# Batch 0's first two token chunks by seven half products, and block-by-block waits for the sums of w_out

## The chip, the core and the metric

The kernel runs on one core of one Trainium2 chip. The metric is the device time of one execution in microseconds (us). The core has five engines that matter here, each with its own in-order queue of instructions: PE (TensorE: matmuls, with the weight loads, PEld, beside them), DVE (VectorE), ACT (ScalarE), POOL (GpSimd) and SP (SyncE, which only issues transfers). An instruction waits at the head of its queue until the semaphores that it names have been raised by others; nothing behind it on that engine starts before it.

## The reference

```python
scores = (1 / sqrt(64)) * q @ k.transpose      # 8 batches, 12 heads, 448 tokens, head size 64
attn   = relu(scores) ** 2 / 448
x      = (attn @ v), heads side by side        # 3584 tokens x 768
h      = x @ w_in                              # w_in 768 x 2048
g      = relu(h) ** 2
out    = g @ w_out                             # w_out 2048 x 768, out 3584 x 768 in float32
```

The inputs come in float32; the kernel casts them to float16 and accumulates in float32.

## The kernel before, in words

**Tiles and stages.** A batch has 448 tokens and 3 units of 4 heads (24 units in all). For each unit, q and k are loaded, cast and turned (`turn_pe` on PE for units 0 to 5, `turn_dma` L476 as a transposing transfer on SP from unit 6 on). A round is one seventh of a unit's keys: `scores` (L522, eight small matmuls of 64x64 tiles for two rounds), then `squared`: the relu out of PSUM into a buffer `rel` (L538 on DVE or L541 on ACT), and its square into `at` (L545 on ACT or L548 on POOL). After seven rounds `av` (L588, 28 small matmuls) gives x, which L608 or L610 writes as `xt`. Then the dense part: `h_group` (L650, six matmuls of 128x128 over 448 columns for each of 16 blocks of w_in; `h_first` at L699 and `h_part` for batch 0), evacuated by ACT (L639, square) and DVE (L634, mask) into `g`.

**The output products.** A token chunk is 128 tokens of `g`, 16 blocks deep. w_out lies in four blocks `w2[hf][i]`: columns `hf` (LO or HI 384), rows `i` (the first or the second 1024). In the names of the code b11 = `w2[0][0]`, b21 = `w2[0][1]`, b12 = `w2[1][0]`, b22 = `w2[1][1]`. One chunk done plainly (`plain_groups`, L799) is two groups of 16 matmuls of 384 columns, one for each half of the columns. Two chunks together can be done by `o_groups` with seven half products (L864), m1 to m7, of 8 such matmuls each, in place of eight: a Strassen-Winograd scheme. It needs four sums of `g` (`combine`, L843, on DVE: s1 to s4) and four sums of w_out (`combine_w2`: t1 = b12-b11, t2 = b22-t1, t4 = t2-b21, and t3 = b22-b12, which is written over b12), each sum of w_out in two halves, on DVE (L828) or POOL (L825). The products' results are put together by ACT copies (L783; L785 is its form on DVE) and DVE additions (`close`, L876), and stored by SP (L745). In the kernel before, 13 of the pairs are done so, and only the first two chunks of batch 0 are plain (`PLAIN0 = True`); since t3 overwrites b12, it waits there for the plain products.

**What sets the order.** The order of each queue is not written by hand. `Plan` records every operation with costs, dependencies, buffers and a due time, then simulates the engines (`simulate`, `pick`: of the operations that are ready, the one with the earliest due time) under 16 pairs of settings (`PATIENCE`, how long PE may idle before a filler matmul, L1009, is put in, and `LEAD`), keeps the best and emits it. `push_dense` queues the dense work of a batch: its 16 h groups mixed with `QUOTA[b]` products that are left over or new; `run_some` spreads that queue between the score rounds. So a small edit can move instructions everywhere. The waits in the emitted program follow from the data that an instruction really touches; the dependencies given to `Plan` only say when the plan takes an operation to be ready.

**Loads.** w_in comes in four transfers on POOL's queue (L496), w_out in four (`load_w2`, L501), in the order of the string `ORDER`, in which w0 to w3 are `w2[0][0]`, `w2[0][1]`, `w2[1][0]`, `w2[1][1]`. On the same queue lie v (L489) and the early q and k (L406). From unit 6 on, q and k are loaded by SP (L389) into four `raw` buffers and cast by POOL (L440) into three `blk` buffers. Where a DVE sum (L828, L843) holds the port that DVE shares with POOL, the next POOL operation of the plan is made to wait for it (`behind`).

Of the kernel before, what the change touches and what calls it, by code (L numbers as in the profile page):

```python
# [297 lines left out]
def kernel(  # L298
# [35 lines left out]
    def fixed(pool, name, n, shape, dt):  # L334
        return [pool.tile(shape, dt, name=f"{name}{i}", tag=f"{name}{i}") for i in range(n)]

    w1 = fixed(sb, "w1_", 4, [P, NM, 512], FP16)
    w2 = [fixed(sb, f"w2_{hf}", 2, [P, NH, HALF], FP16) for hf in range(2)]
    t1, t2, t4 = fixed(sb, "wt", 3, [P, NH, HALF], FP16)
# [160 lines left out]
    def load_w2(hf, i, after, due=None):  # L500
        return plan.add([("POOL", 0.85, 0.85, lambda: nc.gpsimd.dma_start(  # L501
            out=w2[hf][i], in_=moe_w_out[1024 * i:1024 * (i + 1),
                                         hf * HALF:(hf + 1) * HALF].rearrange(
                "(f p) d -> p f d", p=P)), WQ)], after=after, due=due)
# [273 lines left out]
    def copied(op, bank, part):  # L778
        def emit(kind):
            def run():  # L780
                dst, src = part.tile, bank.tile[:, 0:HALF]
                if kind == "ACT":
                    nc.scalar.activation(out=dst, in_=src, func=AF.Copy, scale=CO)  # L783
                else:
                    nc.vector.tensor_scalar_mul(dst, src, CO)  # L785
            return run
        return plan.add([act(HALF, emit("ACT")), dve(HALF, emit("DVE"))], [op], [bank, part],
                        due=plan.now + 0.3)
# [25 lines left out]

    def combine_w2():
        (b11, b21), (b12, b22) = w2
        steps = [("t1", lambda r: (t1[:, r], b12[:, r], b11[:, r]), []),
                 ("t2", lambda r: (t2[:, r], b22[:, r], t1[:, r]), ["t1"]),
                 ("t4", lambda r: (t4[:, r], t2[:, r], b21[:, r]), ["t2"]),
                 ("t3", lambda r: (b12[:, r], b22[:, r], b12[:, r]), ["t1"])]  # L820
        for name, args, before in steps:
            t_ops[name] = [
                plan.add([("POOL", 3.06, 3.1,
                           lambda r=slice(4 * z, 4 * z + 4), args=args:
                           nc.gpsimd.tensor_sub(*args(r))),  # L825
                          ("DVE", 0.9, 0.98,
                           lambda r=slice(4 * z, 4 * z + 4), args=args:
                           nc.vector.tensor_sub(*args(r)), 0, True)],  # L828
                         [w for hf in range(2) for w in w2_ops[hf]]
                         + [t_ops[x][z] for x in before]  # L830
                         + (plain_ops if name == "t3" else []))
                for z in range(2)]

    def o_groups(one, two):
        (ready1, buf1, view1, at1), (ready2, buf2, view2, at2) = one, two
        lo, hi = slice(0, NH), slice(NH, NF)
        st: dict = {}

        def combine(name, fn, deps, srcs, x, y):
            buf = Buf("comb")  # L840

            def emit():
                return fn(buf.tile, x(), y())  # L843
            st[name] = plan.add([("DVE", 0.6, 0.68, emit, 0, True)], deps, [buf] + srcs), buf

        def sums():
            vec = nc.vector
            combine("s1", vec.tensor_add, ready2(), [buf2()],
                    lambda: view2()[:, lo], lambda: view2()[:, hi])
            combine("s2", vec.tensor_sub, ready1() + [st["s1"][0]], [buf1(), st["s1"][1]],  # L850
                    lambda: st["s1"][1].tile, lambda: view1()[:, lo])
            combine("s3", vec.tensor_sub, ready1() + ready2(), [buf1(), buf2()],
                    lambda: view1()[:, lo], lambda: view2()[:, lo])
            combine("s4", vec.tensor_sub, ready1() + [st["s2"][0]], [buf1(), st["s2"][1]],
                    lambda: view1()[:, hi], lambda: st["s2"][1].tile)

        def product(bank, lhs, deps, srcs, w, first, last=True):
            if first:
                st[bank] = Buf("mm")
            buf = st[bank]  # L860

            def emit():
                for j in range(NH):
                    nc.tensor.matmul(  # L864
                        buf.tile[:, 0:HALF], lhsT=lhs()[:, j, :], rhs=w[:, j, :],
                        start=(first and j == 0), stop=(j == NH - 1), skip_group_check=True)
            return plan.pe(0.1625 * NH, emit, deps, [buf] + srcs)

        def part(name, bank, op):
            st[name] = Buf("part")  # L870
            st[name, "op"] = copied(op, st[bank], st[name])
            return st[name, "op"]

        def close(at, cols, bank, op, name, sign=1.0):
            osb, src, r = Buf("part"), st[bank], st[name]
            done = plan.add([dve(HALF, lambda: nc.vector.scalar_tensor_tensor(  # L876
                out=osb.tile, in0=src.tile[:, 0:HALF], scalar=sign * CO, in1=r.tile,
                op0=ALU.mult, op1=ALU.add))], [op, st[name, "op"]], [src, r, osb],
                due=plan.now + 0.3)
            store(done, at, cols, osb)  # L880
            return done

        def summed(name):
            op, buf = st[name]
            return lambda: buf.tile, [op], [buf]

        def m1():
            sums()
            op = product("x", lambda: view1()[:, lo], ready1() + w2_ops[0], [buf1()],
                         w2[0][0], True)  # L890
            part("r1", "x", op)

        def m2():
            op = product("y", lambda: view1()[:, hi], ready1() + w2_ops[0], [buf1()],
                         w2[0][1], True)
            close(at1, LO, "y", op, "r1")

        def m6():
            lhs, deps, srcs = summed("s2")
            op = product("x", lhs, deps + t_ops["t2"] + [st["r1", "op"]], srcs, t2, False)  # L900
            part("r2", "x", op)

        def m5():
            lhs, deps, srcs = summed("s1")
            op = product("z", lhs, deps + t_ops["t1"], srcs, t1, True)
            part("r5", "z", op)

        def m7():
            lhs, deps, srcs = summed("s3")
            op = product("x", lhs, deps + t_ops["t3"] + [st["r2", "op"]], srcs, w2[1][0], False)  # L910
            part("r3", "x", op)
            close(at2, HI, "x", op, "r5")

        def m3():
            lhs, deps, srcs = summed("s4")
            op = product("z", lhs, deps + w2_ops[1] + [st["r5", "op"]], srcs, w2[1][1], False)
            close(at1, HI, "z", op, "r2")

        def m4():
            op = product("w", lambda: view2()[:, hi], ready2() + t_ops["t4"], [buf2()], t4, True)  # L920
            close(at2, LO, "w", op, "r3", -1.0)

        return [(0.1625 * NH, fn) for fn in (m1, m2, m6, m5, m7, m3, m4)]
# [17 lines left out]
            queued -= c  # L941
            credit -= c

    QUOTA = (4, 12, 9, 12, 12, 13, 12, 99)
    backlog: list = []

    def push_dense(b):
# [4 lines left out]
        if b == 0:  # L952
            if PLAIN0:
                both = [plain_groups(chunk(b, c)) for c in range(2)]
# [6 lines left out]
        else:  # L961
# [4 lines left out]
            new += o_groups(chunk(b, 1), chunk(b, 2))  # L966
        old = backlog[:QUOTA[b]]
        beside = max(0, len(old) - 2)
# [11 lines left out]
        backlog[:] = backlog[len(old):] + new  # L980
        now = QUOTA[b] - len(old)
        push(backlog[:now])
        del backlog[:now]
        if b == 0 and PLAIN0:
            push([(0.0, combine_w2)])

    ORDER = "u3 v3 u4 v4 u5 v5 w0 w1 w2 w3"
    EARLY = 6
    PLAIN0 = True
    NPE = 6  # L990
    MERGE = True
    ROUNDS = NUN * TJ
# [77 lines left out]
    tile(1, rounds[0:1])  # L1070
    put(0, quads[-1])
    tile(1, rounds[1:2])
    w2_ops = [[], []]
    for z, one in enumerate(ORDER.split()):
        at, n = 15.0 + 0.01 * z, int(one[1])
        if one[0] == "u":
            for w_ in "kq":
                casts[n, w_] = load_early(n, w_, 15.0, at)
        elif one[0] == "v":
            load_v(n, 15.0, at)  # L1080
        else:
            w2_ops[n // 2].append(load_w2(n // 2, n % 2, 15.0, at))
    for i in range(2, STREAM):
        tile(1, rounds[i:i + 1])
        if i % 4 == 3:
# [1 line left out]
        if i % TJ == 2 and i > TJ:  # L1087
            n = i // TJ - 1
# [12 lines left out]
    for i in range(STREAM // 2, NB):  # L1101
# [19 lines left out]
        for n, t in rs:  # L1121
            sp = [Buf("mm"), Buf("mm")]
            op = scores([(n, t)], sp, WHOLE, False)
# [4 lines left out]
        for op, sp, n, t in todo:  # L1128
            second, at = square(op, sp, S)
# [50 lines left out]
```

## Time and profile before

| what | value |
|---|---|
| six runs | 381.95 to 384.76 us, median 382.55 us |
| the profiled execution | 381.95 us |
| its span, first to last instruction | 380.2 us |
| outside the span | 1.75 us |
| granted TensorE clock, mean | 0.996 |
| fillers L1009 on PE | 20 |
| products L799 / L864 on PE | 64 / 832 matmuls |

The span is what the views show; times in the views count from its start. In the table of groups a matmul's mean is its whole passage; as matmuls are pipelined, the next one starts earlier, and what a matmul costs in a stream is the length of a run of them over their number, which the chain and the timeline give. "idle before" is the time that an engine stood still before an instruction, and the name behind the arrow is what ended it.

### The profile page before, as it was taken

What the parts mean: (1) busy time and instruction counts of PE and PEld (TensorE: products, weight loads), DVE (VectorE), ACT (ScalarE), POOL (GpSimd) and SP (SyncE); (2) the same over time, 40 slices, a digit from 0 to 9 for tenths busy, and PEclk for the clock granted to TensorE, in tenths of its full rate; (3) what the DMA queues carried; (4) which work ended last, traced back from release to release, by engine and by line L of the source; (5) the groups of instructions that cost most, each with busy time, mean ns of one, the idle gap of its engine ahead of it and who ended that gap; (6) DMA issues with size and microseconds to landing.
All of it is one profiled execution on the core that took longest, in us unless ns stands there. A gap on an engine that the chain in (4) does not pass through costs nothing.

```text
span 380.2 us, 8809 instructions
## 1 busy us (share of the span) xinstructions
PE 371.0 (98%) x3295; PEld 198.2 (52%) x3295; DVE 266.3 (70%) x468; ACT 269.8 (71%) x584; POOL 221.5 (58%) x270
## 2 busy tenths in 40 slices
PE   8889999999999999999999999999999999999995
PEld 4546555444555445544554555545555545555663
DVE  2985888786985678677986576685885668256731
ACT  5998999897767787688777686696795785244221
POOL 8999894896756668775475674974752443000100
PEclk9899999999999999999999999999999999999999
DMA  8999998996398954859368764774553002200243
GB/s 183 195 206 203 203 236 214 239 186 153 72 203 192 184 153 80 161 127 242 54 121 219 170 154 83 184 170 103 128 99 84 2 1 60 68 21 0 63 105 85
DMA packets 70219, 51.37 MB, mean 135 GB/s; under 512 B 36896, under 2 KB 70176, under 8 KB 70176
## 3 DMA queue, kind: packets, MB, share of 16 engines
q1 hardware_dynamic: 52384, 35.86, 38.1%
q0 software_dynamic: 16928, 14.09, 25.3%
q10 hardware_dynamic: 864, 0.85, 0.7%
q8 instruction: 26, 0.43, 0.5%
q14 instruction: 17, 0.14, 0.1%
HBM read 45.61 MB, written 11.01 MB: 149 GB/s over the span
## 4 chain that ended last, share of the span: by engine, by line
PE 91%; ACT 3%; POOL 2%; DMA 2%; DVE 1%; issue 0%; POOLq 0%; DVEq 0%; ACTq 0%
PE mm L650 38%; PE mm L864 32%; PE mm L522 9%; PE mm L588 8%; PE mm L799 3%; DMA g<-in_k_dram 2%; POOL at L548 1%; ACT at L545 1%; PE mm L460 1%; ACT rel L541 1%; DVE rel L538 0%; POOL g L406 0%; PE mm L699 0%; PE mm L1009 0%; ACT comb L545 0%
## 5 line engine op out<-in xcount | busy, mean ns | idle before, releaser
L548 POOL TENSOR_TENSOR at<-rel 128x448 f16<-128x448 f32 (+1 forms) x144 | 130.1, 924 | 69.3 <-DVE rel L538 52.3
L650 PE MATMUL mm<-xt,w 128*128 128x448 f16 (+1 forms) x768 | 148.7, 346 | 0.0
L634 DVE SCALAR_TENSOR_TENSOR g<-mm,g 128x448 f16<-128x448 f32 (+1 forms) x128 | 77.2, 605 | 49.9 <-ACT g L639 49.6
L650 PEld LDWEIGHTS <-w 128*128 128x128 f16 x768 | 72.5, 98 | 70.2 <-issue 11.2
L538 DVE TENSOR_SCALAR rel<-mm 128x448 f32<-128x448 f32 (+3 forms) x176 | 97.5, 596 | 13.5 <-PE mm L522 12.6
L639 ACT ACTIVATE g<-mm 128x448 f16<-128x448 f32 (+1 forms) x128 | 68.9, 539 | 46.8 <-PE mm L650 45.5
L545 ACT ACTIVATE at<-rel 128x448 f16<-128x448 f32 (+1 forms) x192 | 101.6, 590 | 0.5 <-PE mm L588 0.5
L541 ACT ACTIVATE rel<-mm 128x448 f32<-128x448 f32 (+2 forms) x172 | 83.1, 548 | 5.3 <-PE mm L522 5.1
L864 PEld LDWEIGHTS <-comb 128*128 128x128 f16 x416 | 39.6, 98 | 30.2 <-issue 4.1
L522 PE MATMUL mm<-qkt,qkt 64*64 64x448 f16 (+2 forms) x756 | 51.6, 341 | 1.1 <-DVE rel L538 0.7
L783 ACT ACTIVATE part<-mm 128x384 f32<-128x384 f32 x42 | 20.9, 498 | 43.9 <-PE mm L864 43.0
L876 DVE SCALAR_TENSOR_TENSOR part<-mm,part 128x384 f32<-128x384 f32 x52 | 28.4, 555 | 24.8 <-ACT part L783 15.0
L440 POOL CAST blk<-raw 128x896 f16<-128x896 f32 x36 | 33.5, 945 | 20.6 <-DMA raw<-in_k_dram 5.4
L864 PE MATMUL mm<-w,comb 128*128 128x384 f16 x208 | 36.7, 326 | 0.0
L864 PE MATMUL mm<-wt,comb 128*128 128x384 f16 x208 | 36.5, 326 | 0.0
L588 PE MATMUL mm<-at,vs 64*64 64x448 f16 (+1 forms) x672 | 35.8, 343 | 0.2
L864 PEld LDWEIGHTS <-g 128*128 128x128 f16 x264 | 25.4, 98 | 18.5 <-issue 1.8
L522 PEld LDWEIGHTS <-qkt 64*64 64x64 f16 x756 | 18.5, 107 | 25.1 <-issue 21.2
L489 POOL DMA_DIRECT2D vs<-in_v_dram x48 | 30.1, 633 | 1.4 <-DMA g<-in_k_dram 1.1
L765 POOL COPY rest<-g 128x1024 f16<-128x1024 f16 x8 | 8.3, 1034 | 38.7 <-DVE comb L843 35.5
L864 PE MATMUL mm<-w,g 128*128 128x384 f16 x176 | 30.8, 326 | 0.0
L588 PEld LDWEIGHTS <-vs 64*64 64x64 f16 x756 | 22.5, 110 | 14.6 <-issue 3.8
(61 smaller groups left out, 211.6 us busy)
## 6 DMA issues: line engine op xcount, KB each, us to landing
out_dram<-part SPq DMA_DIRECT2D x108, 96.0 KB, 2.2
raw<-in_k_dram SPq DMA_DIRECT2D x18, 448.0 KB, 4.1
raw<-in_q_dram SPq DMA_DIRECT2D x18, 448.0 KB, 5.0
vs<-in_v_dram POOLq DMA_DIRECT2D x48, 112.0 KB, 4.4
w<-in_moe_w_in_dram POOLq DMA_DIRECT2D x4, 768.0 KB, 12.5
w<-in_moe_w_out_dram POOLq DMA_DIRECT2D x4, 768.0 KB, 13.6
g<-in_k_dram POOLq DMA_DIRECT2D x4, 224.0 KB, 10.9
g<-in_q_dram POOLq DMA_DIRECT2D x4, 224.0 KB, 10.0
```

The costliest lines, as they stand in the source:

```text
L440: return lambda: fn(blk.tile.rearrange("p t (f d) -> p f t d", f=2), tile_of().rearrange("p f (t d) -> p f t d", d=D))
L489: return lambda: nc.gpsimd.dma_start(out=buf.tile[64 * r:64 * r + 64], in_=src[:, u, hs])
L522: nc.tensor.matmul(sp[e].tile[64 * c:64 * c + 64, c0:c0 + w].rearrange("p (t c) -> p t c", c=TP), lhsT=kT[r, t, 64 * e:64 * e + 64], rhs=q ...
L538: dve(width, lambda: nc.vector.tensor_scalar(out=r.tile[:, 0:width], in0=bank.tile[:, 0:width], scalar1=0.0, scalar2=SK, op0=ALU.max, op1= ...
L541: act(width, lambda: nc.scalar.activation(out=r.tile[:, 0:width], in_=bank.tile[:, 0:width], func=AF.Relu, scale=SK))],
L545: act(width, lambda: nc.scalar.activation(out=dst(), in_=r.tile[:, 0:width], func=AF.Square)),
L548: lambda: nc.gpsimd.tensor_mul(dst(), r.tile[:, 0:width], r.tile[:, 0:width]))],
L588: nc.tensor.matmul(banks[f].tile[64 * e:64 * e + 64, c0:c0 + w], lhsT=vs[r, e ^ c, t * D:(t + 1) * D], rhs=a[r, e, :], start=(t == 0), sto ...
L634: nc.vector.scalar_tensor_tensor(out=dst, in0=src, scalar=0.0, in1=dst, op0=ALU.is_gt, op1=ALU.mult)
L639: nc.scalar.activation(out=dst, in_=src, func=AF.Square)
L650: nc.tensor.matmul(bank.tile[:, c0:c0 + w], lhsT=w1[f // 4][:, m, f % 4 * P:(f % 4 + 1) * P], rhs=xts[b].tile[:, m, cols], start=(m == 0), ...
L864: nc.tensor.matmul(buf.tile[:, 0:HALF], lhsT=lhs()[:, j, :], rhs=w[:, j, :], start=(first and j == 0), stop=(j == NH - 1), skip_group_chec ...
```

## The change

Batch 0's first pair of chunks goes through `o_groups` (seven half products) rather than `plain_groups`. `combine_w2` is queued ahead of batch 0's products; in the plan each sum now depends only on the blocks it reads, and t3's dependence on the plain products falls away with them. m1, m2 and m3 depend in the plan on one block each. The blocks are loaded in the order w0 w2 w3 w1. Two entries of QUOTA rise.

```diff
     def combine_w2():
         (b11, b21), (b12, b22) = w2
-        steps = [("t1", lambda r: (t1[:, r], b12[:, r], b11[:, r]), []),
-                 ("t2", lambda r: (t2[:, r], b22[:, r], t1[:, r]), ["t1"]),
-                 ("t4", lambda r: (t4[:, r], t2[:, r], b21[:, r]), ["t2"]),
-                 ("t3", lambda r: (b12[:, r], b22[:, r], b12[:, r]), ["t1"])]
-        for name, args, before in steps:
+        (o11, o21), (o12, o22) = w2_ops
+        steps = [("t1", lambda r: (t1[:, r], b12[:, r], b11[:, r]), [], [o11, o12]),
+                 ("t2", lambda r: (t2[:, r], b22[:, r], t1[:, r]), ["t1"], [o22]),
+                 ("t4", lambda r: (t4[:, r], t2[:, r], b21[:, r]), ["t2"], [o21]),
+                 ("t3", lambda r: (b12[:, r], b22[:, r], b12[:, r]), ["t1"], [o22] + plain_ops)]
+        for name, args, before, deps in steps:
...
-                         [w for hf in range(2) for w in w2_ops[hf]]
-                         + [t_ops[x][z] for x in before]
-                         + (plain_ops if name == "t3" else []))
+                         deps + [t_ops[x][z] for x in before])
...
-            op = product("x", lambda: view1()[:, lo], ready1() + w2_ops[0], [buf1()],
+            op = product("x", lambda: view1()[:, lo], ready1() + [w2_ops[0][0]], [buf1()],
...
-            op = product("y", lambda: view1()[:, hi], ready1() + w2_ops[0], [buf1()],
+            op = product("y", lambda: view1()[:, hi], ready1() + [w2_ops[0][1]], [buf1()],
...
-            op = product("z", lhs, deps + w2_ops[1] + [st["r5", "op"]], srcs, w2[1][1], False)
+            op = product("z", lhs, deps + [w2_ops[1][1]] + [st["r5", "op"]], srcs, w2[1][1], False)
...
-    QUOTA = (4, 12, 9, 12, 12, 13, 12, 99)
+    QUOTA = (7, 14, 9, 12, 12, 13, 12, 99)
...
-    ORDER = "u3 v3 u4 v4 u5 v5 w0 w1 w2 w3"
+    ORDER = "u3 v3 u4 v4 u5 v5 w0 w2 w3 w1"
     EARLY = 6
-    PLAIN0 = True
+    PLAIN0 = False
...
-    w2_ops = [[], []]
+    w2_ops = [[None, None], [None, None]]
...
-            w2_ops[n // 2].append(load_w2(n // 2, n % 2, 15.0, at))
+            w2_ops[n // 2][n % 2] = load_w2(n // 2, n % 2, 15.0, at)
```

In the changed kernel every line from 830 on has a number lower by one (L864 becomes L863), and L828 becomes L829.

## Prediction

> **What bounds the kernel now.** I read the page's busy shares and its forty slices first, then the chain by line, then the chain in order of time, and last the timelines of the stretch that the change rebuilds.
>
> ```profile
> span 380.2 us, 8809 instructions
> PE 371.0 (98%) x3295; PEld 198.2 (52%) x3295; DVE 266.3 (70%) x468; ACT 269.8 (71%) x584; POOL 221.5 (58%) x270
> ...
> PE   8889999999999999999999999999999999999995
> ...
> PEclk9899999999999999999999999999999999999999
> ```
>
> PE is busy for 98%, and what it lacks lies in the first slices and in the last one. The chain agrees:
>
> ```profile
> PE 91%; ACT 3%; POOL 2%; DMA 2%; DVE 1%; issue 0%; POOLq 0%; DVEq 0%; ACTq 0%
> ```
>
> In order of time it is matmuls alone from 31 us to 376, but for a few short pieces:
>
> ```profile
> 30.52 0.60 PE mm L1009 x4
> 31.11 1.38 PE mm L699 x6
> ...
> 56.25 0.62 DVE rel L538
> ...
> 59.20 7.91 PE mm L799 x48
> 67.11 1.53 PE mm L588 x28
> 68.66 0.55 ACT xt L608
> 69.69 2.76 PE mm L799 x16
> ...
> 96.42 1.24 PE mm L650 x6
> 97.67 2.60 PE mm L864 x16
> ...
> 116.80 1.13 PE mm L650 x6
> 117.93 0.50 PE mm L522 x8
> ...
> 122.44 1.32 PE mm L588 x28
> ```
>
> So a matmul taken away is worth its step, wherever it lay. L699 at 31.11 is the anchor: it needs the last block of w_in, issued at 14.0 us and landed 17.0 us later by the view of L496, at 31.0. Before that PE waits for data; after it PE's own queue is the time.
>
> Two timelines show the little waiting that is left. PE's:
>
> ```profile
> 55.82 0.94 PE L522 MATMUL mm<-qkt,qkt 64*64 64x448 f16 x14
> 56.91 0.38 PE L522 MATMUL mm<-qkt,qkt 64*64 64x448 f16 x2 [0.15 <-DVE rel L538]
> ...
> 68.39 1.29 PE L522 MATMUL mm<-qkt,qkt 64*64 64x448 f16 x16
> ```
>
> and DVE's, with the first sum of w_out and the one long pause of DVE there:
>
> ```profile
> 58.24 1.11 DVE L828 TENSOR_TENSOR wt<-w,w 128x1536 f16<-128x1536 f16 x1
> ...
> 68.63 0.62 DVE L610 TENSOR_SCALAR xt<-mm 128x448 f16<-128x448 f32 x1 [3.06 <-PE mm L588]
> ```
>
> **The change, part by part.**
>
> *Matmuls.* 64 go (L799), 56 come. The step in a stream is 2.60 / 16 = 0.1625 us (L864 at 97.67, entered from other dense work). 8 x 0.1625 = **-1.30 us**, all of it on PE.
>
> *Blocks of small matmuls.* I counted the order of instructions that the changed kernel builds. From the anchor on all other matmuls are there as before, but the score rounds and AV bursts lie in 60 blocks between dense work, not in 56: m7, m3 and m4 of the new pair each stand alone between score rounds. A block costs at both edges. Leaving it: six L650 take 1.24 after a block, 1.13 after dense work, 0.11. Entering it: 28 L588 take 1.32, so 0.047 each, and eight L522 after dense work 0.50 in place of 8 x 0.047 = 0.38, 0.12. 4 x 0.23 = **+0.92 us**.
> The Trainium skill, TensorEngine Tiling (Array Packing), Key Properties, says that changing the tiling mode drains TensorE, which speaks against this change; from TensorE: Matmul & The Clock Gate, Single matmul latency (a fixed 398 cycles at 2.4 GHz), a full drain would be an estimated 0.17 us at each of the 8 new edges, 1.33 us, and the saving would be gone. The rows show 0.11 and 0.12, and they decide.
>
> *Waits on PE between 55 and 70 us.* In the kernel before, two bursts of 16 score matmuls stand there (two pairs of rounds without dense work between), and PE waits in them for PSUM banks: by the starts in the same timeline eight L522 take 0.40 before an AV burst (48.01 to 48.41) and 0.48 behind one (49.73 to 50.21), and eight more take 0.38. So the first burst should take 0.78 and takes 1.10 (55.82 to 56.92), the second 0.86 and takes 1.30 (68.39 to 69.69). Together 0.76 of waiting. In the changed order there is no burst of 16: every pair of rounds from the anchor on has other work on both sides. That could save all of 0.76, or nothing, since ACT is busy for 9.97 of the 10 us from 50 to 60 and the same evacuations remain. I take half, **-0.4 us**, as no row is nearer to one end.
>
> *Fillers.* 10 in place of 20, all before the anchor. The landing of w_in hides them: zero. Bounds: PE starts L699 0.1 after the landing, so -0.1; and if fewer fillers let the clock sink sooner (granted 0.50 from 16 to 18 us in this trace, 1.00 before 12), the 11 transposes before the first scores, 0.056 each, take twice that: +0.6.
>
> *Loads of w_out.* Last in the queue is now b21, not b22. By the view of L501 the four are issued at 35.9, 37.0, 37.8 and 38.7 and land after 9.2, 12.1, 15.0 and 20.7: 45.1, 49.0, 52.8, 59.4. Before, b22 was read by the sixth group of eight of L799, at 59.1 + 5 x 1.3 = 65.6, 6.2 us after it landed. Now b21 is read by the second product, near 59.2 + 1.3 = 60.5: about 1.1 us of cover. Zero, with up to +1.7: SP's loads of q and k run beside the last block, which lands 6.6 us after the third, where the third lands 3.8 after the second; if the third were slowed alike, the last would land at 62.2.
>
> *DVE.* From 58.24 to 68.63 it works 7.33 of 10.39 us and pauses 3.06. Added there: s1 to s4 (0.85, 0.68, 0.85, 0.81, the rows of L843), t3 whole (2 x 0.98; POOL loses its half of 3.13 at 75.5), one `close` (0.56): 5.71. Gone: the first half of t1, now done as soon as the first two blocks are in (1.11), and one L610 that goes to ACT (0.61). Net +4.0 against 3.06; but the next scores stand behind m7, 1.3 us later, so it fits by 0.4 us. The products' needs come in time: s1 near 60 for a product at 61.7, s2 near 63.5 for one at 65.5, t3 and s3 near 66.6 for m7 at 68.2. Behind these sums on DVE's queue wait the relus of the next scores, and on POOL's the cast for the last transpose of unit 7: it waits for t4, at about 69. Then 0.9 for the cast, and transposes land 3.2 to 6.3 us after their issue in this trace: 73.3 to 76.4, for scores that come near 76. I take +0.1 for all this, between 0 and 0.4 here, and keep the rest for the rivals.
>
> *Small things.* 4 more L783 on ACT, 4 more L876, 4 fewer L785 on DVE; POOL has two more squares. The last 264 dense matmuls (L650 x96, L864 x168) and the end behind them stand as before: zero.
>
> **Sum.** -1.30 + 0.92 - 0.4 + 0.1 = -0.7 us; against the profiled execution 381.95 - 0.7 = 381.25 (span 379.5 and 1.75 around it). The median of the six runs is 0.6 above that execution, so I forecast a median of **381.85**, a gain of 0.2%. About 0.3%, 1.15 us, is what a measurement of this kernel tells from no change.
>
> **Rivals.**
>
> *Faster: the waits of that stretch go altogether.* Besides the two bursts, L588 at 56.92 took 1.56 (1.32 alone) and L522 at 58.48 took 0.66 (0.48): 0.42 more. If spreading the rounds ends all four, -1.30 + 0.92 - 0.76 - 0.42 = -1.56: 381.0. For it: they all lie within two crowded stretches. Against: ACT has no pause there.
>
> *Slower: DVE becomes the bound between 58 and 76 us.* Its ten sums stand nearly in a row, and behind them four `close` (4 x 0.56) beside relus where the kernel before had one copy (0.56) and a half of t3 (0.98), 0.7 more. If the 1.3 us that m7 gives is not there because PE waits elsewhere, the excess is 0.94, with the closes 1.65; one of the closes also waits for a store that SP issues behind a transpose, and such a store took 5.3 us to land (65.64 to 70.93) where the median is 2.2, which may add 1. So a wait on PE of 0.94 to 2.65, -0.38 with it: it decides from 1.5 us of lateness on. I take 2.2, so +1.8: 384.35. Against: every need above is met with over a microsecond by the rows.
>
> *Level: the block b21 comes late.* It decides from a landing past 60.5; 1 us late gives -0.7 + 1.0 = +0.3: 382.85.
>
> *The change does not do what it says,* in that the waits only move: -1.30 + 0.92 = -0.38, 382.15; it lies in the forecast's own spread.
>
> **How the numbers follow.** Forecast with that spread 0.57, faster rival 0.20, DVE 0.15, late block 0.08. Faster by over 0.3%: 0.16 of the faster rival, 0.05 of the forecast, 0.21. Slower: 0.13 of the DVE rival, 0.02 of the late block, 0.02 of the forecast (fillers), 0.17. Within: 0.62. The range takes in the faster rival with the spread of runs, the bounds +0.6 and +1.7 and the lower half of the DVE rival: 380.8 to 384.2.
>
> **What would show it.** In the profile after: L864's successor with 896 matmuls and no L799; the anchor still near 31.0; no 16 scores in a row; the edges still 0.11 and 0.12; PE's end near 375.3 in place of 376.0. Wrong would be a PE wait on a sum (wt or comb) or on the last w_out block near 60, a PE wait on a relu of DVE near 70, or a wait on a transpose near 76; or a new wait far from here, as the plan moves the order of all later batches too.

## The result, and the profile after

The changed kernel takes **380.5 us** (median of 16 runs, 379.26 to 382.1) against 382.47 for the kernel before (37 runs beside it): a ratio of 0.9948, 95% interval 0.9935 to 0.996. That is faster by 0.5%, about 1.97 us, and lies below the range of the prediction (380.8 to 384.2). One run of the experiment e4 below, 544.69 us at a granted clock of 0.656, is left out of its ratio. The profiled execution took 380.25 us, 378.5 of it the span.

The page after shows the same picture as before: PE busy nearly everywhere, the clock full, and again only the first and the last slices short.

```profile
span 378.5 us, 8791 instructions
PE 368.4 (97%) x3277; PEld 195.0 (52%) x3277; DVE 272.3 (72%) x468; ACT 272.8 (72%) x592; POOL 219.6 (58%) x270
...
PE   6889999999999999999999999999999999999995
...
PEclk9999999999999999999999999999999999999998
...
PE 91%; DMA 5%; POOL 1%; ACT 1%; issue 0%; DVE 0%; POOLq 0%
```

PE's busy time fell by 2.6 us while its share fell, so a share of busy time does not tell the gain. What tells it is the stretch behind the anchor (the fourth L699 group, which waits for the last block of w_in). I split it for every run in the same way: each run of matmuls in the timeline against its steps as the kernel before has them (0.1625 us for 384 columns and so on, and 0.23 for each block of small matmuls); what a run of matmuls takes beyond that is a **wait**. So the waits are a remainder: they hold whatever the price of 0.23 leaves over. By this split the kernel before has 792 matmuls of 384 columns, 56 blocks and 2.34 us of waits in 344.95 us from the anchor (31.02) to PE's end (375.97). The changed kernel has 784, 60 and 0.78 us in 343.0 us, from 31.25 to 374.25. (Its 784 are all in L863, 14 pairs of 56. The prediction named 896 as the sign, and the table of the kernel before has 832 for L864; the trace of the kernel before has 728, 13 pairs of 56. The 8 fewer are as forecast.) So the sum reads -1.30 + 0.92 - 1.56 = -1.94, and +0.23 because the last block of w_in landed at 31.20, not 30.98.

PE's timeline of the rebuilt stretch in the changed kernel (columns: start, length, engine, line, tiles, shape, count):

```profile
56.65 0.57 PE L522 MATMUL mm<-qkt,qkt 64*64 64x448 f16 x8
57.05 1.49 PE L588 MATMUL mm<-at,vs 64*64 64x448 f16 x28
58.38 0.55 PE L522 MATMUL mm<-qkt,qkt 64*64 64x448 f16 x8
58.86 2.77 PE L863 MATMUL mm<-w,g 128*128 128x384 f16 x16
61.47 1.46 PE L863 MATMUL mm<-wt,comb 128*128 128x384 f16 x8
62.77 2.76 PE L863 MATMUL mm<-w,g 128*128 128x384 f16 x16
65.37 1.46 PE L863 MATMUL mm<-wt,comb 128*128 128x384 f16 x8
66.76 1.52 PE L588 MATMUL mm<-at,vs 64*64 64x448 f16 x28
68.24 1.48 PE L863 MATMUL mm<-w,comb 128*128 128x384 f16 x8
69.65 0.57 PE L522 MATMUL mm<-qkt,qkt 64*64 64x448 f16 x8
70.15 1.47 PE L863 MATMUL mm<-w,comb 128*128 128x384 f16 x8
71.56 0.57 PE L522 MATMUL mm<-qkt,qkt 64*64 64x448 f16 x8
72.11 1.46 PE L863 MATMUL mm<-wt,g 128*128 128x384 f16 x8
73.50 0.57 PE L522 MATMUL mm<-qkt,qkt 64*64 64x448 f16 x8
```

At this place the kernel before has:

```profile
56.92 1.90 PE L588 MATMUL mm<-at,vs 64*64 64x448 f16 x28
58.48 0.72 PE L522 MATMUL mm<-qkt,qkt 64*64 64x448 f16 x8
```

In the changed kernel there is no burst of 16 scores and no bracket, that is, no idle time. Read by starts: 28 L588 take 57.05 to 58.38, 1.33, where the kernel before took 56.92 to 58.48, 1.56; m3, alone between score rounds, takes 70.15 to 71.56, 1.41, which is 8 x 0.1625 + 0.11; the score round ahead of it takes 0.50. Both edges are as forecast. m7, at 68.24, now stands between the AV burst and the next scores.

DVE over the same stretch works without a pause worth the name, and still nobody on PE waits for it:

```profile
58.69 1.43 DVE L829 TENSOR_TENSOR wt<-w,w 128x1536 f16<-128x1536 f16 x1
60.04 0.68 DVE L842 TENSOR_TENSOR comb<-g 128x1024 f16<-128x1024 f16 x1
...
61.71 2.54 DVE L829 TENSOR_TENSOR wt<-w,wt 128x1536 f16<-128x1536 f16 x2
...
68.71 1.82 DVE L829 TENSOR_TENSOR wt<-wt,w 128x1536 f16<-128x1536 f16 x2
70.45 1.15 DVE L538 TENSOR_SCALAR rel<-mm 128x448 f32<-128x448 f32 x2
```

The first sum takes 1.43 us, where the two of its size at 68.71 take 1.82 together. That is a first sign of what the later experiments show.

### The profile page after: what moved, and what is told of

Read it like the earlier page. It is cut to its first block, busy times and chain, and to the rows that moved or that the text cites. A ratio compares the mean times of both kernels' runs of the same rounds, so it can differ in the third digit from the quotient of the medians.

```text
span 378.5 us, 8791 instructions
## 1 busy us (share of the span) xinstructions
PE 368.4 (97%) x3277; PEld 195.0 (52%) x3277; DVE 272.3 (72%) x468; ACT 272.8 (72%) x592; POOL 219.6 (58%) x270
## 4 chain that ended last, share of the span: by engine, by line
PE 91%; DMA 5%; POOL 1%; ACT 1%; issue 0%; DVE 0%; POOLq 0%
PE mm L650 38%; PE mm L863 34%; PE mm L522 9%; PE mm L588 8%; DMA w<-in_moe_w_in_dram 3%; DMA g<-in_k_dram 2%; PE mm L460 1%; PE mm L699 1%; POOL comb L548 1%; ACT at L545 1%; POOL vs L489 0%; ACT g L729 0%; POOL w L496 0%; ACT rel L541 0%; PE mm L1008 0%
## 5 line engine op out<-in xcount | busy, mean ns | idle before, releaser
L548 POOL TENSOR_TENSOR at<-rel 128x448 f16<-128x448 f32 (+1 forms) x147 | 132.0, 918 | 69.7 <-DVE rel L538 48.1
L538 DVE TENSOR_SCALAR rel<-mm 128x448 f32<-128x448 f32 (+3 forms) x174 | 96.7, 595 | 18.3 <-PE mm L522 17.3
L634 DVE SCALAR_TENSOR_TENSOR g<-mm,g 128x448 f16<-128x448 f32 (+1 forms) x128 | 77.2, 605 | 45.4 <-ACT g L639 45.2
L545 ACT ACTIVATE at<-rel 128x448 f16<-128x448 f32 (+1 forms) x189 | 100.4, 588 | 0.8 <-PE mm L588 0.5
L541 ACT ACTIVATE rel<-mm 128x448 f32<-128x448 f32 (+2 forms) x174 | 84.4, 548 | 5.7 <-PE mm L522 5.7
L863 PEld LDWEIGHTS <-comb 128*128 128x128 f16 x448 | 42.6, 98 | 32.3 <-issue 4.7
L783 ACT ACTIVATE part<-mm 128x384 f32<-128x384 f32 x46 | 22.8, 504 | 38.8 <-PE mm L863 38.7
L875 DVE SCALAR_TENSOR_TENSOR part<-mm,part 128x384 f32<-128x384 f32 x56 | 30.4, 553 | 19.4 <-ACT part L783 12.0
L863 PE MATMUL mm<-w,comb 128*128 128x384 f16 x224 | 39.5, 327 | 0.0
L863 PE MATMUL mm<-wt,comb 128*128 128x384 f16 x224 | 39.4, 326 | 0.0
L863 PEld LDWEIGHTS <-g 128*128 128x128 f16 x288 | 27.6, 98 | 20.6 <-issue 2.8
L588 PE MATMUL mm<-at,vs 64*64 64x448 f16 (+1 forms) x672 | 35.2, 343 | 0.2
L863 PE MATMUL mm<-w,g 128*128 128x384 f16 x192 | 33.7, 326 | 0.0
L588 PEld LDWEIGHTS <-vs 64*64 64x64 f16 x756 | 21.9, 107 | 14.1 <-issue 3.0
```

The costliest lines, as they stand in the source:

```text
L538: dve(width, lambda: nc.vector.tensor_scalar(out=r.tile[:, 0:width], in0=bank.tile[:, 0:width], scalar1=0.0, scalar2=SK, op0=ALU.max, op1= ...
L541: act(width, lambda: nc.scalar.activation(out=r.tile[:, 0:width], in_=bank.tile[:, 0:width], func=AF.Relu, scale=SK))],
L545: act(width, lambda: nc.scalar.activation(out=dst(), in_=r.tile[:, 0:width], func=AF.Square)),
L548: lambda: nc.gpsimd.tensor_mul(dst(), r.tile[:, 0:width], r.tile[:, 0:width]))],
L588: nc.tensor.matmul(banks[f].tile[64 * e:64 * e + 64, c0:c0 + w], lhsT=vs[r, e ^ c, t * D:(t + 1) * D], rhs=a[r, e, :], start=(t == 0), sto ...
L634: nc.vector.scalar_tensor_tensor(out=dst, in0=src, scalar=0.0, in1=dst, op0=ALU.is_gt, op1=ALU.mult)
```

## The experiments

Every ratio is against the kernel before, in runs beside it. The other columns are the split above, from the one profiled execution of each. In these the anchor lay between 30.39 us (e1) and 32.40 (e10), so lengths from the anchor are compared, not ends. Three of the profiled executions are not typical of their runs: those of e1 (381.87 us) and e14 (379.55) are the fastest, that of e10 (383.11, median 380.8) the slowest.

| run | 384-column matmuls | blocks | waits, us | anchor to PE's end, us | ratio, 95% interval |
|---|---|---|---|---|---|
| before | 792 | 56 | 2.34 | 344.95 | 1 |
| after | 784 | 60 | 0.78 | 343.00 | 0.9948, 0.9935 to 0.996 |
| e1 finer waits only | 792 | 56 | 1.97 | 344.45 | 1.0015, 0.9999 to 1.0032 |
| e2 seven products only | 784 | 65 | 2.52 | 345.98 | 1.0021, 1.0008 to 1.0034 |
| e3 seven and quotas | 784 | 59 | 2.78 | 344.76 | 0.9976, 0.9963 to 0.9989 |
| e4 plain in halves | 792 | 57 | 5.80 | 348.62 | 1.0053, 1.0032 to 1.0074 |
| e5 before, 8 fewer | 784 | 56 | 3.84 | 345.14 | 1.0007, 0.9986 to 1.0027 |
| e6 after, m7 later | 784 | 59 | 2.09 | 344.07 | 0.994, 0.9919 to 0.9961 |
| e7 after, coarse waits | 784 | 59 | 2.70 | 344.68 | 0.9973, 0.9957 to 0.999 |
| e8 after, old load order | 784 | 62 | 2.05 | 344.59 | 0.9973, 0.9957 to 0.9988 |
| e9 after, 8 more | 792 | 60 | 0.79 | 344.31 | 0.9974, 0.996 to 0.9988 |
| e10 after, first 8 fewer | 776 | 60 | 3.80 | 344.73 | 0.9958, 0.9941 to 0.9976 |
| e11 before, 8 fewer late | 784 | 56 | 2.68 | 343.99 | 0.9972, 0.995 to 0.9993 |
| e12 e5, loads behind | 784 | 56 | 3.50 | 344.80 | 0.9996, 0.9974 to 1.0018 |
| e13 after, POOL busy | 784 | 60 | 2.80 | 345.09 | 0.9972, 0.9947 to 0.9998 |
| e14 after, last 8 fewer | 776 | 60 | 1.70 | 342.60 | 0.994, 0.9916 to 0.9965 |
| e15 e14, less POOL | 776 | 60 | 1.71 | 342.62 | 0.9913, 0.9888 to 0.9938 |
| e16 e12, less POOL | 784 | 56 | 2.89 | 344.20 | 0.9969, 0.9947 to 0.999 |

In the texts on record "theory A" stands at first for the prediction's account of the waits (they come with bursts of 16 scores), and from e9 on for its other premise, that a matmul is worth its step wherever it lies.

**The parts alone.** e1 keeps the plain products, the old load order and the old quotas, and has only the finer waits. e2 has only the seven products, e3 the seven products and the new quotas; both with coarse waits and the old order of loads.

```diff
e1: the hunks of the change in combine_w2, m1, m2, m3 and w2_ops, nothing else
e2:
-    PLAIN0 = True
+    PLAIN0 = False
e3: e2 and
-    QUOTA = (4, 12, 9, 12, 12, 13, 12, 99)
+    QUOTA = (7, 14, 9, 12, 12, 13, 12, 99)
```

> The kernel before with one part of the change: sums of w_out and products depend in the plan on the blocks that they read; batch 0's first pair stays plain, load order and quotas as before. Matmuls 64 plain, 56 blocks of small matmuls behind the anchor, both bursts of 16 score matmuls still there, 10 fillers. Theory A (the gain is 8 matmuls less, 0.23 us for each block more, and the waits of PE on score banks that go with the bursts of 16): no change, 0.0 us against before, and PE waits of about 2.4 us behind the anchor stay. Rival C (the gain comes from the finer waits in the plan): about -1.6 us. Rival B (any new plan loses the waits by luck): somewhere between 0 and -1.6, with waits gone although the bursts are there.

> The kernel before with seven half products for the first pair alone; coarse dependencies, load order and quotas as before. 56 matmuls for the pair, 65 blocks of small matmuls (9 more than before), no burst of 16. Theory A: -1.30 + 9 x 0.23 - 1.6 = -0.8 us against before, waits behind the anchor under 1 us. Rival C: the waits stay, -1.30 + 2.07 = +0.8 us. If an edge cost the estimated full drain of the page on TensorE (0.33 for a block): -1.30 + 3.0 - 1.6 = +0.1 us.

> As the one with seven products alone, and the two quotas of the change as well; dependencies and load order as before. 56 matmuls, 59 blocks (3 more than before), no burst of 16. Theory A: -1.30 + 0.69 - 1.6 = -2.2 us against before, 1.4 us below the kernel with seven products alone (6 blocks x 0.23). Rival C: -0.6 us. At 0.33 for a block it would lie 2.0 us below the kernel with seven products alone.

The finer waits alone bring nothing (1.0015), and the seven products alone do not either (1.0021): their 8 matmuls are paid back by 65 blocks. The quotas make 59 of the 65 and bring 0.0045 of the ratio, 1.7 us, where 6 x 0.23 is 1.4. Neither run has a burst of 16 in the rebuilt stretch, and both have waits there all the same, so "waits come with bursts of 16" falls as the whole account. In e2 PE waits for a copy of x by DVE (0.40 us, L610) and for a relu of DVE (0.43, L538). PE's timeline of e3:

```profile
66.44 1.52 PE L588 MATMUL mm<-at,vs 64*64 64x448 f16 x28
67.79 0.36 PE L522 MATMUL mm<-qkt,qkt 64*64 64x448 f16 x4
68.66 0.62 PE L522 MATMUL mm<-qkt,qkt 64*64 64x448 f16 x4 [0.51 <-ACT xt L608]
69.22 1.47 PE L864 MATMUL mm<-w,comb 128*128 128x384 f16 x8
```

By this view the last four scores behind the AV burst wait for ACT's L608, the copy that empties a bank of PSUM which this very burst filled. In the changed kernel m7 stands in between, and its 1.3 us cover the copy. Not every round of scores behind an AV burst waits: the one at 58.38 in the changed kernel has no product ahead of it and takes its usual 0.48.

**Taking the parts back from the changed kernel.** e6 emits m7 behind the next two score rounds; e7 has the changed kernel with the coarse waits for the sums; e8 has it with the old order of loads.

```diff
e6: m7 and what depends on it moved behind the next two rounds of scores
e7:
-                         deps + [t_ops[x][z] for x in before])
+                         [w for hf in range(2) for w in w2_ops[hf]] + (plain_ops if name == "t3" else [])
+                         + [t_ops[x][z] for x in before])
e8:
-    ORDER = "u3 v3 u4 v4 u5 v5 w0 w2 w3 w1"
+    ORDER = "u3 v3 u4 v4 u5 v5 w0 w1 w2 w3"
```

> The changed kernel with one move on PE: m7 of the new pair, which stands between the second AV burst behind the products and the next pair of score rounds, is put behind these rounds; all else in the plan's order. Theory A (waits come from bursts of 16) has fallen, since both kernels with seven products and no such burst waited for 2.5 to 2.8 us. Theory D: the wait near 68 us comes from the two score banks that the AV burst has just filled and that the xt evacuation (0.55 us each, on ACT or DVE) must empty; a product behind the AV burst hides it. D: a PE wait of 0.5 to 0.9 us at these scores, one block less (-0.23), so +0.3 to +0.7 us against the changed kernel. If a product there hides nothing: -0.2 us.

> The changed kernel, but in the plan each sum of w_out again waits for all four blocks; load order, quotas and the products' own waits are as changed. PE's order near the products becomes that of the kernel with seven products and the new quotas: score rounds directly behind the AV burst, 59 blocks. Theory D: the wait of about 0.9 us behind the AV burst is back and the rest as there, so about 1.0 us above the changed kernel, 0.8 us below before. If the finer waits of the sums do nothing: level with the changed kernel, or 0.2 below it by the one block less.

> The changed kernel with the w_out blocks loaded in the old order w0 w1 w2 w3. 62 blocks (2 more than the changed kernel), one burst of 16 scores ahead of the products, and products directly behind both AV bursts. Theory D: +0.46 for the blocks, no wait behind the AV bursts, 0.3 in the burst of 16: +0.8 us against the changed kernel. If the load order were what matters (its last block is read 1.1 us after it lands): a wait of PE on the last block that is not there in the changed kernel, and over +1 us.

e7 and e8 each lose about half of the gain: both 0.9973 against 0.9948, 0.96 us. In both, waits are back on PE, 2.70 and 2.05 us. In e8 a burst of 16 scores is back, with 0.67 us, 0.66 us more stand behind the scores of 73.07, and two blocks more cost 0.46 at 0.23 each; in e7 the scores stand right behind the second AV burst again, with m7 behind them, and 0.52 us of its waits are for the last w_out block, which landed at 60.50 in that execution and which e7's edit does not touch. e6 shows the bank wait again in its timeline, 0.46 us put down to ACT's L626 (the same copy as L608), and 1.07 us more behind the anchor. But its runs do not show it: 0.994, 0.3 us below the changed kernel (between 1.2 below and 0.6 above), where 0.3 to 0.7 above was forecast. So by time the bank wait is not confirmed. PE's timelines of e7, e8 and e6:

```profile
69.37 0.43 PE L522 MATMUL mm<-qkt,qkt 64*64 64x448 f16 x4 [0.51 <-ACT xt L608]
...
74.11 1.29 PE L650 MATMUL mm<-xt,w 128*128 128x448 f16 x6 [0.50 <-ACT rel L541]
```

```profile
56.70 1.00 PE L522 MATMUL mm<-qkt,qkt 64*64 64x448 f16 x14
57.85 0.38 PE L522 MATMUL mm<-qkt,qkt 64*64 64x448 f16 x2 [0.15 <-DVE rel L538]
...
74.24 1.46 PE L863 MATMUL mm<-wt,g 128*128 128x384 f16 x8 [0.60 <-DVE rel L538]
```

```profile
68.45 0.81 PE L540 MATMUL mm<-qkt,qkt 64*64 64x448 f16 x4 [0.46 <-ACT xt L626]
```

The waits go with the order on PE, not with the execution. Read by starts, those of the kernel before between 55 and 70 us (0.32 and 0.44 in the bursts, 0.23 and 0.18 between) recur within 0.01 us in e5, e12 and e16, which keep PE's order there; e9, e10, e13, e14 and e15, which keep the changed kernel's order, have none of the four.

**Another way to save the waits.** e4 keeps the plain products of 16 matmuls but cuts them into halves of 8, one for each w_out block, so that they can lie between score rounds as the seven do.

```diff
-                    for f in range(NF):
+                    for f in range(NH * z, NH * z + NH):
...
-    QUOTA = (4, 12, 9, 12, 12, 13, 12, 99)
+    QUOTA = (8, 12, 9, 12, 12, 13, 12, 99)
```

> The kernel before with the first pair still plain, 64 matmuls, but each group of 16 queued as two halves of 8 (first quota 8, as there are 8 pieces), so that score rounds can stand between them; dependencies per block for these products alone. 57 blocks, one burst of 16 left in place of two. Theory A: no matmul saved, one block more (+0.23), about half of the waits between 55 and 70 us gone (-0.6), the later ones as the plan has them: -0.4 us, between 0 and -1.4. If the gain of the change is all in the matmuls: +0.2 us.

It is slower, 1.0053, where 0.4 us of gain was forecast. Unit 7's scores came at 73.9 us and its transposed k and q only at 75.86 and 76.44:

```profile
76.57 0.38 PE L522 MATMUL mm<-qkt,qkt 64*64 64x448 f16 x4 [2.30 <-DMA qkt<-blk]
```

**Is a matmul worth its step?** e5 is the kernel before with 2 of the 16 matmuls left out of each of the four plain groups, 8 fewer; its output lacks those blocks' part.

```diff
-                    for f in range(NF):
+                    for f in [z for z in range(NF) if z not in (7, 8)]:
```

> The kernel before with every queue in the same order, but each of the four plain groups of the first pair leaves out 2 of its 16 matmuls (blocks 7 and 8 of the chunk's depth, so those contributions are missing from the output of these two chunks). It prices the matmuls by themselves: 8 x 0.1625 = -1.30 us against before if PE is the bound throughout and the waits near 68 us hang on things that move with PE (banks that wait for the AV burst). If those waits hang on a transfer or on another engine's own queue, the matmuls saved turn into a longer wait: between -1.3 and 0.

**Nothing was gained** (1.0007, 0.9986 to 1.0027). In PE's timeline the whole saving stands as one wait, at the scores of unit 7:

```profile
71.95 1.31 PE L650 MATMUL mm<-xt,w 128*128 128x448 f16 x6
73.19 0.38 PE L522 MATMUL mm<-qkt,qkt 64*64 64x448 f16 x4
74.89 0.38 PE L522 MATMUL mm<-qkt,qkt 64*64 64x448 f16 x4 [1.31 <-DMA qkt<-blk]
```

In the kernel before the same scores begin at 74.12, with the transposes landed at 74.09: no wait in the profile, and hardly any cover either.

```profile
74.12 0.57 PE L522 MATMUL mm<-qkt,qkt 64*64 64x448 f16 x8
```

The landing is the bound that the prediction did not see, since it shows nowhere as waiting.

e9, e10 and e11 repeat that test elsewhere: 8 matmuls more in the changed kernel (m4 of the first pair computed twice), 8 fewer in it (m1 and m2 from half of their blocks), and 8 fewer late in the kernel before, at 213.8 and 218.4 us.

```diff
e9:
...
+        return range(2 * NH if len(made) == 7 else NH)
...
e10:
...
+        return range(NH // 2 if len(made) in (1, 2) else NH)
...
e11 (kernel before):
...
+        return range(NH // 2 if len(made) in (36, 37) else NH)
...
```

> The changed kernel with one of the seven half products (m4 of the first pair) computed twice, 8 dense matmuls more in the stretch from 66 to 74 us; one sum of the output counts m4 twice. Theory D (a matmul has its price of 0.1625 us only where PE is the bound; in the changed kernel PE is the bound there, with cover left behind it): +1.3 us against the changed kernel, so 381.8 and -0.7 against the kernel before. Rival (some other engine has become the bound in that stretch and PE has slack): under +0.5, 381.0 or less.

> The changed kernel with the first two half products of the first pair computed from half of their blocks, 8 dense matmuls fewer ahead of unit 7's scores; its output lacks those parts. Theory A (a matmul is worth its step wherever it lay): -1.3 against the changed kernel, 379.2. Theory D: the same, as unit 7's transposes had landed 2.1 us ahead of their first use in the changed kernel, and only 0.03 us ahead in the kernel before, where the same cut gave nothing. Rival E (in this stretch, in whatever order, something else stands right behind PE): nothing, 380.5.

> The kernel before with 8 matmuls left out of a pair late in the run (half of the blocks of two half products near 240 us), where its output lacks those parts. Theory D: -1.3 against the kernel before (381.2), since PE has no wait there and nothing stands close behind it; the same cut in the first pair gave 0. Theory E (8 matmuls are too few to show anywhere, other work always fills the place): 0 to -0.4.

e9: 344.31 against 343.00 behind the anchor, +1.31, as 8 x 0.1625 says, and 0.9974 against 0.9948, +1.0 us. So in the changed kernel PE is the bound there, and matmuls added cost their step. Taken away they are not worth it. e10 is no faster than the changed kernel (0.9958). In its profile, which is of its slowest run, PE waits at the second product for the last w_out block, which landed at 62.40 in this execution, and then 1.26 us at the second pair, at 102 us; what holds its median is not shown by that.

```profile
60.01 0.82 PE L869 MATMUL mm<-w,g 128*128 128x384 f16 x4
62.44 0.82 PE L869 MATMUL mm<-w,g 128*128 128x384 f16 x4 [1.61 <-DMA w<-in_moe_w_out_dram]
```

e11 keeps 0.96 of 1.30 behind the anchor; a wait of 0.44 at the AV burst just behind the second cut, 0.24 of it put down to DVE's g (L634), where it was 0.10, takes the rest. By time it is -1.07 us (-0.27 to -1.9). So late in the run most of the step is gained, in the first pair none.

**Where the saving goes next.** e12 is e5 with unit 8's loads of q and k put behind unit 7's transposes on SP's queue, and unit 8's first cast three instructions later on POOL.

```diff
 SP:
-L389 raw<-k, raw<-q (unit 8)
...
 L476 qkt<-blk x2 (unit 7)
+L389 raw<-k, raw<-q (unit 8)
```

> The kernel before with the 8 matmuls of the first, plain pair left out, as in the experiment that gave nothing, and also unit 8's loads of q and k put behind unit 7's transposes on SP's queue (unit 8's first cast put three instructions later on POOL). Theory D (the saving was eaten by unit 7's transposes, which land late behind those loads): the wait of 1.5 us near 73 us falls under 0.5, and the time is 0.8 to 1.3 below the kernel before. Rival (the transposes are late for their cast's sake, which waits for a sum on DVE and POOL): the wait stays over 1 us and the time stays at the kernel before's.

Unit 7's transposes now landed at 71.86 and 72.74, and the wait of 1.5 us at 73 is gone. But the time did not follow (0.9996): 1.06 us of wait appeared at the second pair, near 100 us, behind DVE's sums, of which the second and third took 1.42 us each where 0.68 is their usual length. PE's and DVE's timelines of e12:

```profile
101.52 1.47 PE L894 MATMUL mm<-wt,comb 128*128 128x384 f16 x8 [0.72 <-DVE comb L873]
```

```profile
98.11 0.68 DVE L873 TENSOR_TENSOR comb<-g 128x1024 f16<-128x1024 f16 x1
98.71 1.42 DVE L873 TENSOR_TENSOR comb<-g,g 128x1024 f16<-128x1024 f16 x1
100.05 1.42 DVE L873 TENSOR_TENSOR comb<-comb,g 128x1024 f16<-128x1024 f16 x1
```

and POOL's, with two squares of 0.93 us each stretched to 2.71 together:

```profile
98.30 1.27 POOL L468 CAST blk<-raw 128x896 f16<-128x896 f32 x1 [2.24 <-DMA raw<-in_q_dram]
99.54 2.71 POOL L578 TENSOR_TENSOR at<-rel 128x448 f16<-128x448 f32 x2
```

Four more runs ask whether POOL is the cause. e13 adds work: in the changed kernel, in a pause of POOL beside those sums, one copy is made three times over. e16 takes work away: e12 with those two squares cut from 448 to 64 columns, which its output lacks. e14 is the changed kernel with m3 and m4 from half of their blocks (8 matmuls fewer, behind the last w_out block; its output lacks them), and e15 the same with the two squares cut.

```diff
e13:
...
+                for _ in range(3 if (pr, i) == (0, 1) else 1):
+                    got = nc.gpsimd.tensor_copy(buf.tile[:, :, 64 * i:64 * i + 64],
...
e14:
...
+        return range(NH // 2 if len(made) in (6, 7) else NH)
...
e15, e16:
...
+        n = 64 if len(squares) in (54, 55) else src.shape[-1]
+        return nc.gpsimd.tensor_mul(dst[:, 0:n], src[:, 0:n], src[:, 0:n])
...
```

> The changed kernel, with one copy of POOL (the rest columns of batch 1, 1.03 us at 99.3 us) done three times over, in a pause of POOL of 2.2 us that stands beside DVE's sums for the second pair; same output. Theory P (POOL and DVE's two-input sums keep each other waiting): the sums from 100.0 us on take about 1.4 us in place of 0.68, the product that reads the third sum waits about 1.0 us (0.7 to 1.3), and the time is 0.7 to 1.3 above the changed kernel, 381.5. Rival (the sums' length has another cause, POOL's work is hidden): sums of 0.68, time as the changed kernel, 380.5.

> The changed kernel with its last two half products of the first pair (m3 and m4) computed from half of their blocks, 8 dense matmuls fewer; its output lacks those parts. Theory A (a matmul is worth its step wherever it lay): -1.3 against the changed kernel, 379.2. Theory P: the second pair comes 1.3 us earlier to sums that POOL's squares and copy then hold up; a PE wait of 0.7 to 1.3 stands there near 100 us, and the time is 380 to 380.5.

> The same with two of POOL's squares just ahead of the second pair's sums cut from 448 columns to 64 (about 0.7 us less each on POOL); the output lacks those too. Theory P: the wait near 100 us falls by at least 0.6 us and the time to 379.2 to 379.8. Theory A and any rival in which POOL does not matter: as the run without that cut.

> The kernel before with 8 matmuls of the first pair left out and unit 8's loads put behind unit 7's transposes, where the wait had moved from 73 us to 99.3 us (1.06 us), now also with the two squares of POOL that ran beside the sums there cut from 448 to 64 columns; output lacks those. Theory P: the second and third sum fall from 1.42 towards 0.68, the wait from 1.06 to under 0.4, and the time to 0.9 to 1.3 under the kernel before (381.2). Rival (POOL does not matter): wait and time as without the cut, 382.0.

e13's profile did as forecast by theory P (POOL and DVE's sums keep each other waiting). DVE, POOL and PE in it:

```profile
100.83 0.86 DVE L844 TENSOR_TENSOR comb<-g 128x1024 f16<-128x1024 f16 x1
101.61 1.52 DVE L844 TENSOR_TENSOR comb<-g,g 128x1024 f16<-128x1024 f16 x1
103.06 1.52 DVE L844 TENSOR_TENSOR comb<-comb,g 128x1024 f16<-128x1024 f16 x1
```

```profile
100.11 3.92 POOL L766 COPY rest<-g 128x1024 f16<-128x1024 f16 x3
```

```profile
104.63 1.47 PE L865 MATMUL mm<-wt,comb 128*128 128x384 f16 x8 [0.52 <-DVE comb L844]
```

In the changed kernel these three sums took 0.86, 0.68 and 0.68. The wait of PE there is 1.03 us. By time e13 lies 0.9 us above the changed kernel (0.9972), but the two intervals overlap, so the runs alone do not show it. Its profiled execution has a second wait, 0.89 us at 61.03 for the last w_out block (landed at 60.99, in the changed kernel's profile at 59.56); that one is not POOL's.

e16: the second and third sum fell from 1.42 to 0.78, while the first, now beside a cast of POOL, rose from 0.68 to 1.37. PE's wait at these products fell from 1.06 to 0.10 (0.20 more at the scores ahead of them). DVE's timeline of e16:

```profile
99.53 1.37 DVE L880 TENSOR_TENSOR comb<-g 128x1024 f16<-128x1024 f16 x1
100.83 0.78 DVE L880 TENSOR_TENSOR comb<-g,g 128x1024 f16<-128x1024 f16 x1
101.52 0.78 DVE L880 TENSOR_TENSOR comb<-comb,g 128x1024 f16<-128x1024 f16 x1
```

The time is 0.9969 of the kernel before, 1.2 us under it (0.4 to 2.0), and 0.75 us under it behind the anchor. So of the 1.3 us that e5 took away from PE, between half and nearly all came back, and only when **two further bounds** had been moved: the transposes, and POOL beside DVE's sums. That the second of them mattered rests on the profiles, as the intervals of e12 and e16 overlap.

e14 and e15 settle less. e14 is about as fast as the changed kernel (0.994, 0.3 us less, within the noise; 0.40 less behind the anchor), so its 8 matmuls too were not worth their 1.3 us. But its wait is not at the second pair, as theory P had it: 0.69 and 0.28 us stand at the scores at 70.6 and 72.5, which m3 and m4 had covered. e15 ran at 0.9913, yet its profile has the same waits as e14's and the same length behind the anchor (342.62 against 342.60); the two intervals overlap, so whether its runs gained anything over e14's stays open.

## Why the prediction was wrong

**Right.** Matmuls: -1.30, confirmed by count and by e9. Blocks: 60, at 0.11 and 0.12 for the edges. The Trainium skill says in TensorEngine Tiling (Array Packing), Key Properties, that a change of tiling mode drains TensorE. The timeline shows these 0.11 and 0.12 us for it, and not the 0.17 that the prediction estimated for a full drain from the page TensorE: Matmul & The Clock Gate, Single matmul latency. The fillers, 10 in place of 20, cost nothing: the anchor followed the landing of w_in by 0.05 us. No burst of 16.

**Wrong: the step "waits on PE between 55 and 70 us", taken as -0.4, with +0.1 for DVE beside it.** It measured -1.56 in all: the 1.19 us of that stretch went altogether, as the first rival had it, and another 0.6 us at 223 to 281 us went besides; no sum was waited for, so the +0.1 was zero. The kind of wait was right, PE waiting for ACT or DVE to empty a bank of PSUM, and the bursts of 16 are one place where it stands: every one in these profiles carries a wait. But they are not the only place. e2, e3, e6 and e7 wait without a burst, and in the kernel before 0.42 us of the 1.19 lay outside the bursts.

The reason for "half" was that ACT is busy for 9.97 of the 10 us from 50 to 60. ACT is busy for 9.97 of these 10 us in the changed kernel too, and PE is busy for all 10.00 of them, where it was for 9.83: a busy engine that empties PSUM need not hold PE up, if other work stands between. The prediction's own chain had the path, AV burst (67.11), ACT's copy L608 (68.66), products (69.69). In the changed kernel m7 stands behind that burst, and its 1.3 us are longer than each of the waits. The finer waits and the new load order, with the products and the quotas, brought PE's new order about: without the one or the other half of the gain is lost, and waits are back (e7, e8). That m7's place is what does it is read from the profiles of e3, e6 and e7; the runs of e6 do not confirm it. The 0.6 us at 223 to 281 us are absent from every run with seven products, e2 included. Their largest part, 0.32, stood at scores right behind an AV burst (281.04 to 281.84, 0.80 in place of 0.48). In the changed kernel the same scores stand right behind the same burst, at 279.64 to 280.12, and do not wait, so no product in between can be the reason here; what is stays open. First the kernel before, then the changed one:

```profile
281.04 0.87 PE L522 MATMUL mm<-qkt,qkt 64*64 64x448 f16 x8
```

```profile
279.64 0.55 PE L522 MATMUL mm<-qkt,qkt 64*64 64x448 f16 x8
```

**Wrong too: "a matmul taken away is worth its step, wherever it lay".** The chain of matmuls alone from 31 to 376 us supports a price for matmuls added. For matmuls taken away it supports nothing, since a bound with no cover leaves no wait to see: e5 gained nothing, e10 and e14 nothing clear of noise, e11 most. In the change the -1.30 was kept, as its other parts moved the next bounds as well; this is read from the profile, not tested alone: unit 7's scores came at 76.4 us in place of 74.1, behind transposes that had landed at 71.83 and 74.49.

**The rivals.** DVE did not become the bound: its sums ran in a row from 58.69 to 70.45, as its rival feared, and PE waited for none. The late block b21 did not come late in the profiled execution, with 0.6 us of cover and not the 1.1 forecast; but in other executions with the same order of loads the second product waited for it, 0.52 us in e7, 0.89 in e13 and 1.61 in e10 (there with four matmuls fewer ahead of it). The runs of the changed kernel lie 2.8 us apart, and this may be one thing that parts them; no run shows it.

## What to carry to other kernels

Before a saving on the busiest engine is put into a sum, list what stands close behind it: for each instruction of that engine, how long its last input had been there, from the landings and ends of the others. A price measured by adding work holds for adding only; to price a removal, remove something as cheap to try as two matmuls of a group. And where PE waits for a bank that its own previous burst filled, look for work that can be put between the two before looking for a faster evacuation.

## What the runs showed of the hardware

- DVE's sums of two float16 tiles in SBUF (128x1024) take 0.68 us with POOL at rest, and 1.42 (e12) or 1.52 (e13) with POOL at work on SBUF beside them; lengths between occur as well (0.78 in e16). In e12 POOL's squares beside them take 1.37 in place of 0.93, in turns with them. DVE's relus, one input from PSUM, took 0.61 to 0.63 whatever POOL did. The Trainium skill says in SBUF — State Buffer, Who interferes with whom, that a DVE instruction with two SBUF inputs contends with a POOL instruction that reads SBUF, and that the port pair they share is an exclusive lock. The runs agree: POOL's copies made three times over (e13) lengthened the second and third sum, and POOL's squares cut short (e16) shortened them.
- A transposing transfer of a unit took 2.9 us from issue to landing at best and up to 6.3 in the kernel before. Unit 7's took 5.39 and 4.10 in e12, with unit 8's loads put behind them, in place of 6.31 and 6.01 in e5.
- The last w_out block, issued between 38.0 and 40.1 us in all these profiles, landed between 58.04 (e5) and 62.40 us (e10), 19.4 to 22.3 us after its issue.
